# Attention in two groups per unit ahead of two feed-forward layers: rounds, corner masks, GpSimd low parts and early products

## The chip, the cores and the metric

The kernel runs on one core of a Trainium2 chip. The metric is the device time of one execution in microseconds. Before the change the median of three runs was 858.65 us (858.62 to 858.83).

## The reference

Three stages follow each other; everything is float32.

```python
# attention: 4 batches, 8 heads, 576 positions, 64 dimensions; stride 32
scores = q @ k.transpose(0, 1, 3, 2) / np.sqrt(64)
rel = pos[:, None] - pos[None, :]
mask_local = (rel >= 0) & (rel < 32)                                  # heads 0 to 3
mask_strided = (rel >= 0) & (pos[None, :] % 32 == pos[:, None] % 32)  # heads 4 to 7
attn = softmax(where(mask, scores, -1e9)) @ v
x = attn as 2304 tokens x 512
h = x @ w_in                       # 512 x 2048
y = (h * np.cos(h)) @ w_out        # 2048 x 512
g = y @ w_gate; val = y @ w_val    # 512 x 1536 each
out = (g / (1 + np.exp(-g)) * val) @ w_out2   # 1536 x 512
```

## The kernel before

**Engines.** TensorE multiplies; VectorE, ScalarE and GpSimd do what lies between; SP issues all loads, in the order in which the program writes them. Each engine works through its own instructions in the written order. The order is made by hand, in Python, by the loops below.

**Attention.** A unit is a batch with a pair of heads, either local or strided; 16 units, taken in pairs of one strided and one local unit. A local unit has nine blocks of 64 queries against 96 keys, a strided one eleven of 54 against 54. A unit is cut into three groups (`groups`, L78): three blocks each if local, four, four and three if strided. The loop at L813 runs in rounds. A round starts one group, strided and local in turn, so that a pair of units takes six rounds, and it takes the groups that were started earlier one step on: the sums, transpositions, values and puts of groups that are 2, 5, 6 and 7 rounds old (`LAGS`). The steps of a group: `scores` (TensorE; each float32 multiplication is two instructions in the trace, and the two heads lie in two 64x64 corners of the array; then a filler multiplication `hot` into unused columns, and one with an identity that adds the mask), `top` (VectorE's maximum, which GpSimd scales), `exps` (ScalarE), `sums` (VectorE), `norm` (VectorE's reciprocal, GpSimd's product), `transposes` (TensorE), `evac` (ScalarE), `values` (TensorE), `put` (ScalarE). Behind the last group, rounds go on for the older steps; these are the attention's tail. There TensorE gets a filler (`keep_warm`) or half of the first product of `x @ w_in`.

**Filler work.** `later` queues steps with a cost in units of about 1 us of VectorE, and `pump(share)` emits as many as a round's or slot's share allows; `need(key)` emits all that stands ahead of a key. In the attention the queue holds, for each of the 16 chunks of w_in, a conversion to float32 with a maximum (`conv_steps`: ScalarE, then VectorE); then the common scale; then the split of each chunk into a 16-bit high part (`hi`, ScalarE) and low part (`lo`, VectorE), with a scan of a chunk of w_out beside each. Chunk j+2's tile holds chunk j in float32 until j is split. Chunks (512 KB) arrive in six `raw` buffers; a step that frees one issues the next load. Loads of w_out wait for `RELEASE`.

**First layer.** `up1` multiplies block 0 to 4 of the tokens (512 or 384) with chunk m of w_in: 4 x 3 multiplications, high and low parts. A slot is one such product. On its result work `up1_a` (ScalarE, into one of four `tb` buffers), `up1_b` (VectorE), `up1_c` (ScalarE, the sine), `up1_d` (VectorE; frees the PSUM bank) and `up1_e` (ScalarE rounds, GpSimd subtracts for the low part; frees `tb`). The second multiplication, `down1` with w_out, starts at slot `HEAD`, and from there catches up at `RATE`. `direct_later` splits w_out beside it and scans w_gate and w_val. In slots ahead of `HEAD`, PSUM's four `acc` banks serve as further homes of products.

**Second layer.** It follows with the same weights' splits and isn't touched.

## Time and profile before

| | before |
|---|---|
| median of three runs | 858.65 us |
| the profiled execution's own time | 859.65 us |
| its span, first to last instruction | 858.0 us |
| TensorE busy | 844.9 us, 98% |
| VectorE, ScalarE, GpSimd busy | 653.6, 520.4, 200.0 us |
| TensorE's granted clock, mean | 1.000 |
| read from memory, written | 177.05, 23.99 MB |

A busy TensorE is not a TensorE at its peak: its instructions overlap, and the time between the starts of two is what one costs. So in the timeline below the difference of two rows' first column is read, not the second. The attention takes the first 100 us of the span; slot 16, where the second block begins, starts at 141 us.

### The profile page before, as it was taken

Reading aid. Unit: us, or ns where it says so; the run is one execution under the profiler, and the core shown is the slowest. Engines: PE = TensorE matmul, PEld = TensorE weight load, DVE = VectorE, ACT = ScalarE, POOL = GpSimd, SP = SyncE. Lnnn points to the kernel's source line nnn. Section 1 sums busy time; section 2 is a strip of 40 time slices with the busy share of each in tenths; the row PEclk is TensorE's granted clock in tenths of the full one; section 3 lists DMA queues with packets and bytes.
Section 4 is the critical chain, followed back from the end, with each engine's and each line's share of the span. In section 5 each row is a group of like instructions: output and inputs, shape, how many; then the busy total and the mean of one; then the engine's idle time right before and its main releaser. Section 6 shows DMA issues by size and latency. Waiting matters only on the chain.

```text
span 858.0 us, 18338 instructions
## 1 busy us (share of the span) xinstructions
PE 844.9 (98%) x7223; PEld 601.9 (70%) x7223; DVE 653.6 (76%) x1256; ACT 520.4 (61%) x1047; POOL 200.0 (23%) x281
## 2 busy tenths in 40 slices
PE   9999999999999999999999999999999999999998
PEld 5777544444444444555666788888888899999998
DVE  6999989997888978789996378567756765765562
ACT  6899889554657766768885466545344444444440
POOL 3454234211445546423223100000000000000000
PEclk9999999999999999999999999999999999999999
DMA  9998822897567566514356257667777688789894
GB/s 364 408 381 274 280 90 78 282 337 260 167 198 240 198 214 205 178 34 177 131 193 249 75 194 282 230 218 263 235 262 239 238 273 289 280 306 319 323 321 145
DMA packets 53605, 202.21 MB, mean 236 GB/s; under 512 B 5264, under 2 KB 15888, under 8 KB 49680
## 3 DMA queue, kind: packets, MB, share of 16 engines
q1 hardware_dynamic: 53520, 201.06, 67.3%
q8 instruction: 56, 0.92, 0.4%
q14 instruction: 29, 0.24, 0.1%
HBM read 177.05 MB, written 23.99 MB: 234 GB/s over the span
## 4 chain that ended last, share of the span: by engine, by line
PE 83%; DVE 11%; DMA 2%; ACT 2%; issue 1%; POOL 0%; SPq 0%; ACTq 0%; POOLq 0%
PE acc L734 14%; PE bank L581 13%; PE bank L582 12%; PE bank L583 12%; PE acc L583 7%; PE acc L581 7%; PE acc L582 7%; PE bank L466 3%; PE po L523 2%; DMA raw<-w_val 2%; DVE tb L624 1%; DVE tb L617 1%; PE tp L501 1%; DVE cv L265 1%; PE bank L468 1%
## 5 line engine op out<-in xcount | busy, mean ns | idle before, releaser
L581 PE MATMUL bank<-xs,wi 128*128 128x256 f16 (+3 forms) x776 | 231.1, 298 | 4.4 <-DVE q L145 1.7
L583 PE MATMUL bank<-xs,wi 128*128 128x256 f16 (+3 forms) x776 | 231.1, 298 | 0.0
L582 PE MATMUL bank<-xs,wi 128*128 128x256 f16 (+3 forms) x776 | 231.1, 298 | 0.0
L629 POOL TENSOR_TENSOR arena<-tb,arena 128x512 f16<-128x512 f32 (+1 forms) x80 | 91.5, 1144 | 239.6 <-ACT arena L628 212.9
L582 PEld LDWEIGHTS <-wi 128*128 128x128 f16 x880 | 86.1, 98 | 41.5 <-issue 7.2
L583 PE MATMUL acc<-arena 128*128 128x512 f16 (+1 forms) x320 | 114.5, 358 | 0.5 <-DVE arena L278 0.5
L581 PE MATMUL acc<-arena 128*128 128x512 f16 (+1 forms) x320 | 114.5, 358 | 0.0
L582 PE MATMUL acc<-arena 128*128 128x512 f16 (+1 forms) x320 | 114.5, 358 | 0.0
L581 PEld LDWEIGHTS <-wi 128*128 128x128 f16 x880 | 86.1, 98 | 36.0 <-issue 1.1
L583 PEld LDWEIGHTS <-wi 128*128 128x128 f16 x880 | 86.1, 98 | 34.7
L734 PEld LDWEIGHTS <-arena 128*128 128x128 f16 x1080 | 100.7, 98 | 8.1
L719 POOL TENSOR_TENSOR wi<-tb 128x256 f32<-128x256 f32 (+1 forms) x30 | 20.2, 675 | 338.5 <-DVE tb L701 338.5
L704 ACT ACTIVATE arena<-tb 128x256 f16<-128x256 f32 (+3 forms) x59 | 28.6, 485 | 99.0 <-DVE tb L701 90.6
L1228 DVE TENSOR_TENSOR arena<-bank,cv 128x512 f32<-128x512 f32 (+1 forms) x60 | 37.9, 636 | 66.0 <-PE bank L583 66.0
L583 PEld LDWEIGHTS <-arena 128*128 128x128 f16 x600 | 58.7, 98 | 33.7 <-DVE arena L278 1.0
L734 PE MATMUL acc<-arena 128*128 128x256 f16 (+1 forms) x702 | 82.0, 265 | 0.0
L582 PEld LDWEIGHTS <-arena 128*128 128x128 f16 x600 | 58.7, 98 | 32.6
L581 PEld LDWEIGHTS <-arena 128*128 128x128 f16 x600 | 58.7, 98 | 32.4
L628 ACT ACTIVATE arena<-tb 128x512 f16<-128x512 f32 (+1 forms) x80 | 46.6, 583 | 53.5 <-PE acc L583 51.9
L614 ACT ACTIVATE tb<-bank,quarter,c 128x512 int32<-128x512 f32 (+1 forms) x74 | 53.7, 725 | 33.7 <-PE bank L583 25.5
L701 DVE SCALAR_TENSOR_TENSOR tb<-tb,c,arena 128x512 f32<-128x512 f32 (+1 forms) x60 | 41.7, 695 | 35.8 <-ACT tb L696 35.8
L1224 ACT ACTIVATE cv<-bank 128x512 f32<-128x512 f32 (+1 forms) x90 | 49.3, 548 | 30.1 <-PE bank L583 29.1
(143 smaller groups left out, 1722.3 us busy)
## 6 DMA issues: line engine op xcount, KB each, us to landing
wi<-w SPq DMA_DIRECT2D x20, 1792.0 KB, 7.7
arena<-w SPq DMA_DIRECT2D x60, 576.0 KB, 4.9
raw<-w_out SPq DMA_DIRECT2D x56, 512.0 KB, 4.7
arena<-w SPq DMA_DIRECT2D x10, 1792.0 KB, 8.9
raw<-w_gate SPq DMA_DIRECT2D x24, 512.0 KB, 4.2
raw<-w_val SPq DMA_DIRECT2D x24, 512.0 KB, 5.6
w<-arena SPq DMA_DIRECT2D x42, 256.0 KB, 3.0
raw<-w_in SPq DMA_DIRECT2D x16, 512.0 KB, 9.1
```

The lines of the kernel that those rows point to most:

```text
L466: nc.tensor.matmul(out=self.sc[r, i, :], lhsT=qk_t[self.i][r, q0:q0 + 64], rhs=qk_t[self.i][r, k0:k0 + w], start=i == 0, stop=False)
L581: nc.tensor.matmul(out=o, lhsT=w[:, 0, c], rhs=x[0], start=first, stop=False, **kw)
L582: nc.tensor.matmul(out=o, lhsT=w[:, 0, c], rhs=x[1], start=False, stop=False, **kw)
L583: nc.tensor.matmul(out=o, lhsT=w[:, 1, c], rhs=x[0], start=False, stop=last, **kw)
L614: nc.scalar.activation(out=c["w"].bitcast(I32), in_=c["ph"], func=AF.Identity, scale=turn[c["blk"]], bias=quarter)
L628: nc.scalar.activation(out=g[:, 0, 0:n], in_=w, func=AF.Copy)
L629: nc.gpsimd.tensor_tensor(out=g[:, 1, 0:n], in0=w, in1=g[:, 0, 0:n], op=ALU.subtract)
L701: nc.vector.scalar_tensor_tensor(out=t, in0=t, scalar=s_g[c["blk"]], in1=c["C"][m][:, 1, 0:c["n"]], op0=ALU.mult, op1=ALU.mult)
L704: nc.scalar.activation(out=to, in_=src, func=AF.Copy, scale=2.0 ** -11)
L734: nc.tensor.matmul(out=o[:, c], lhsT=w[:, 256 * i + 128 * c:256 * i + 128 * c + 128], rhs=unit(u)[:, x:x + h], start=j == c == i == 0, sto ...
L1224: nc.scalar.activation(out=t, in_=src, func=AF.Copy)
L1228: nc.vector.tensor_tensor(out=c["C"][m][:, :, h * right:h * right + h], in0=p, in1=t, op=ALU.add)
```

## The change

Units are cut into two groups (five and four blocks if local, six and five if strided), so a pair of units takes four rounds instead of six. The lags are 2, 4, 5 and 6. In `scores` the filler comes first and has the columns that the group leaves free; the mask is added by two multiplications, each in the corner of its head. In a round, scores come ahead of transpositions, exponentials ahead of evictions, and VectorE's maximum stands between two halves of the filler work. A strided and a local group share one tile of sums and one reciprocal. There are three tiles of exponentials of each kind instead of four. The values of a pair of units are loaded in its first round, before they were in the round ahead of it. The low parts of w_in's odd chunks are made on GpSimd in two instructions. In the tail four whole first products are multiplied instead of one in halves. Shares and limits of the filler work have other numbers. `AHEAD` is 0 and adds only three empty steps.

```diff
-LAGS = (2, 5, 6, 7)
+LAGS = (2, 4, 5, 6)
+ROUND = 4
-PUMP, KP = 1.05, 8
+PUMP, PUMP_END, KP = 1.25, 2.2, 5
-EARLY, K0 = 1, 1
-HEAD, HSHARE = 16, 0.8
-RATE, MINLAG = 0.7, 2
+EARLY, K0 = 4, 2
+HEAD, HSHARE = 17, 0.8
+RATE, MINLAG = 0.75, 2
-RELEASE = 30
+RELEASE = 18
...
-    return [(0, 3), (3, 3), (6, 3)] if is_local(p) else [(0, 4), (4, 4), (8, 3)]
+    return [(0, 5), (5, 4)] if is_local(p) else [(0, 6), (6, 5)]
...
+            def lo_pool(mat, j, tiles):
+                c = as_f32(tiles[j + 2])
+                nc.gpsimd.tensor_scalar(out=c, in0=c, scalar1=scale_w[mat][0], scalar2=1.0, op0=ALU.mult, op1=ALU.mult)
+                nc.gpsimd.tensor_tensor(out=tiles[j][:, 1], in0=c, in1=tiles[j][:, 0], op=ALU.subtract)
+
             def lo(mat, j, tiles):
-                later(0.7, lambda: lo_part(tiles[j][:, 1], as_f32(tiles[j + 2]), scale_w[mat][0], tiles[j][:, 0]), (mat, j))
+                if j % 2:
+                    later(0, lambda: lo_pool(mat, j, tiles), (mat, j))
+                else:
+                    later(0.7, lambda: lo_part(tiles[j][:, 1], as_f32(tiles[j + 2]), scale_w[mat][0], tiles[j][:, 0]), (mat, j))
...
+                nc.tensor.matmul(out=b[:, n * w:512], lhsT=ones16, rhs=hot[:, 0:512 - n * w], start=True, stop=False)
...
-                nc.tensor.matmul(out=b[:, 288:512], lhsT=ones16, rhs=hot[:, 0:224], start=False, stop=False)
-                nc.tensor.matmul(out=self.sc, lhsT=id16, rhs=mask, start=False, stop=True)
+                for h in range(2):
+                    r = slice(64 * h, 64 * h + 64)
+                    nc.tensor.matmul(out=self.sc[r], lhsT=id16[r, r], rhs=mask[r], start=False, stop=True)
...
             if group(LAGS[0]):
-                group(LAGS[0]).sums()
+                mate = group(LAGS[0] + 1)
+                group(LAGS[0]).sums(mate)
+                if group(LAGS[0]).loc:
+                    group(LAGS[0]).invert()
+                    mate.norm()
+                    group(LAGS[0]).norm()
+            if group(0):
+                group(0).scores()
+            begun = k - len(gs) - K0
+            if 0 <= begun < EARLY:
+                need(("in", begun))
+                early = up1(0, begun)
...
+            share = 0 if k < KP else PUMP if group(0) else PUMP_END
+            pump(share * 0.5)
+            if group(0):
+                group(0).top()
+                if g == 0 and i >= 4:
+                    load_v(i)
+                    load_v(i + 1)
...
+            pump(share * 0.5)
```

TensorE, two rounds in the middle of the attention, as the program orders them: first a local round of before, from its transpositions on (`tp`; `bank` holds scores, `po` values, `fix` the masks). A float32 multiplication is one row here and two instructions in the trace.

```order
L505 MATMUL tp<-fix,e_s_100 128x128 x2
L466 MATMUL bank<-qkl 64x96 x6
L468 LDWEIGHTS ones_77
L468 MATMUL bank<-hot,ones_77 128x224
L469 LDWEIGHTS id_76
L469 MATMUL bank<-fix,id_76 128x288
L523 MATMUL po<-pt,vl 64x64 x6
```

And a local round of the change:

```order
L472 MATMUL bank<-hot,ones_77 128x32
L478 MATMUL bank<-qkl 64x96 x10
L482 LDWEIGHTS id_76
L482 MATMUL bank<-fix,id_76 64x480
L482 LDWEIGHTS id_76
L482 MATMUL bank<-fix,id_76 64x480
L521 MATMUL tp<-fix,e_l_103 96x128 x5
L541 MATMUL po<-pts,v_pair_107 64x54 x12
```

Of what was three rounds' work of a unit two rounds are left; the filler stands first and is short, and the mask is in two halves of 64 partitions.

ScalarE in the attention's tail, from the first high parts of w_in on (`wi<-wi`; `xy<-po` are puts, `pt` and `pts` evictions, `tb` the first steps of products). Before:

```order
L275 ACTIVATE wi<-wi,s_1681 128x512 x2
L545 ACTIVATE xy_68<-po 128x8x12
L545 ACTIVATE xy_69<-po 128x8x6
L512 ACTIVATE pts<-tp 128x256
L481 ACTIVATE e_s_98<-bank,mx 128x54 x3
L275 ACTIVATE wi<-wi,s_1681 128x512
L536 ACTIVATE xy_69<-po 128x192
L512 ACTIVATE pt<-tp 96x384
L481 ACTIVATE e_l_102<-bank,mx 128x96 x3
L545 ACTIVATE xy_69<-po 128x12x6
```

With the change:

```order
L278 ACTIVATE wi<-wi,s_1688 128x512 x4
L554 ACTIVATE xy_70<-po 128x256
L530 ACTIVATE pt<-tp 96x384
L530 ACTIVATE pt<-tp 96x256
L278 ACTIVATE wi<-wi,s_1688 128x512 x2
L563 ACTIVATE xy_69<-po 128x18x6
L563 ACTIVATE xy_70<-po 128x18x12
L530 ACTIVATE pts<-tp 128x384
L632 ACTIVATE tb<-bank,quarter,c_1770 128x512
L278 ACTIVATE wi<-wi,s_1688 128x512 x2
L554 ACTIVATE xy_69<-po 128x192
L554 ACTIVATE xy_70<-po 128x128
```

The first high parts stood ahead of groups that still had their exponentials to come; now they stand behind all exponentials, more of them per round, and among the first products' steps.

SP's loads ahead of the third pair of units' values (`v_pair`, `vl`), from the fourth pair's queries and keys on (`qks`, `qkl`). Before:

```order
L432 DMA qks<-qk_s 128x1188
L432 DMA qkl<-qk_l 128x1184
L195 DMA raw<-w_in 128x1024 x2
L443 DMA v_pair_108<-v_s 64x768 x2
L439 DMA vl<-v_l 128x1152
```

With the change:

```order
L443 DMA qks<-qk_s 128x1188
L443 DMA qkl<-qk_l 128x1184
L198 DMA raw<-w_in 128x1024 x2
L443 DMA qks<-qk_s 128x1188
L443 DMA qkl<-qk_l 128x1184
L198 DMA raw<-w_in 128x1024
L454 DMA v_pair_106<-v_s 64x768 x2
L450 DMA vl<-v_l 128x1152
```

The fifth pair's queries and keys and one more chunk of w_in have moved ahead of the values.

## Rows read from the trace of the kernel before

**Rows 1.** Windows: stretch, its length, busy us (instructions) per engine, clock, DMA share, GB/s

```profile
20.00:90.00 70.00, 69.93 (x1177) 50.40 (x1173) 66.67 (x192) 65.03 (x245) 34.99 (x75) 1.00 0.94 351
141.00:208.00 67.00, 65.51 (x303) 29.51 (x303) 63.36 (x110) 37.97 (x60) 13.76 (x13) 1.00 0.84 294
```

**Rows 2.** Chain of waits: start us, us, engine, tile, line

```profile
71.80 0.52 PE po L523 x12
...
111.71 0.78 ACT tb L614
...
113.08 1.16 POOL arena L629
114.30 0.78 ACT tb L614
```

**Rows 3.** TensorE's timeline: two rounds from 42.99 us; start, us, instructions

```profile
42.99 0.56 PE L466 MATMUL bank<-qks 64*64 64x54 f32 x12
43.48 0.27 PE L468 MATMUL bank<-hot,ones 128*128 128x224 bf16 x1
43.59 0.23 PE L469 MATMUL bank<-fix,id 128*128 128x162 bf16 x1
43.75 0.56 PE L523 MATMUL po<-pts,v_pair 108*64 108x54 f32 x12
44.24 0.44 PE L505 MATMUL tp<-fix,e_s 128*128 128x128 f32 x2
44.61 0.71 PE L466 MATMUL bank<-qkl 64*64 64x96 f32 x12
...
46.54 0.67 PE L466 MATMUL bank<-qks 64*64 64x54 f32 x16
47.14 0.27 PE L468 MATMUL bank<-hot,ones 128*128 128x224 bf16 x1
```

**Rows 4.** Last two score multiplications of 43 us; line L466's durations (min/median/max ns)

```profile
43.32 0.23 PE L466 MATMUL bank<-qks 64*64 64x54 f32 x2
...
L466 PE MATMUL bank<-qks x12: 218/218/258, 43.0 to 43.3; 64*64 64x54 f32 x12
```

**Rows 5.** TensorE's timeline: the first scores, and the first instruction behind the last round

```profile
6.43 1.10 PE L466 MATMUL bank<-qks 64*64 64x54 f32 x16
...
91.26 0.33 PE L811 MATMUL bank<-fix,id 128*128 128x384 bf16 x1
```

**Rows 6.** DMA, 0 to 100 us: GB/s in 40 slices of 2.5 us; loads, KB each

```profile
GB/s 57 385 380 405 412 420 420 400 415 406 406 408 404 407 410 409 405 412 404 416 401 410 314 264 411 416 372 197 288 243 164 228 321 331 308 246 231 228 257 297
...
raw<-w_in SPq DMA_DIRECT2D x16, 512.0 KB, 9.1
qks<-qk_s SPq DMA_DIRECT2D x8, 594.0 KB, 8.6
...
vl<-v_l SPq DMA_DIRECT2D x8, 576.0 KB, 7.4
v_pair<-v_s SPq DMA_DIRECT2D x16, 192.0 KB, 6.6
```

**Rows 7.** ScalarE's timeline from 104.73 us

```profile
104.73 1.28 ACT L621 ACT_TABLE_LOAD   x1
...
106.65 0.76 ACT L614 ACTIVATE tb<-bank,quarter,c 128x512 int32<-128x512 f32 x1
107.32 0.71 ACT L275 ACTIVATE wi<-wi,s 128x512 f16<-128x512 f32 x1
107.93 0.71 ACT L621 ACTIVATE tb<-tb,right 128x512 f32<-128x512 f32 x1
```

**Rows 8.** VectorE's timeline: two low parts of w_in, the second beside GpSimd

```profile
91.35 0.74 DVE L278 SCALAR_TENSOR_TENSOR wi<-wi,s 128x512 f16<-128x512 f32 x1
92.01 0.68 DVE L204 TENSOR_REDUCE pw_out<-raw 128x1 f32<-128x512 f32 x1
...
92.95 1.18 DVE L278 SCALAR_TENSOR_TENSOR wi<-wi,s 128x512 f16<-128x512 f32 x1
```

More of the change, by code (lines that the diff above doesn't have):

```diff
@@ L164, in build @@
         beside = {j: [] for j in range(M1)}
+        ahead = [("gate", j) for j in range(AHEAD)]
         for i, key in enumerate((mat, j) for mat in ("gate", "val") for j in range(M2)):
-            beside[ALONE + i * (M1 - ALONE) // (2 * M2)].append(key)
-        order = deque([("in", j) for j in range(M1)] + [("out", j) for j in range(M1)]
+            if key not in ahead:
+                beside[ALONE + i * (M1 - ALONE) // (2 * M2)].append(key)
+        order = deque([("in", j) for j in range(M1)] + [("out", j) for j in range(M1)] + ahead
                       + [key for j in range(M1) for key in [("out", j)] + beside[j]]
@@ L774, in quarter_out @@
                 store("12", 0, h)
-        gs = [Group(i + d, g) for i in range(0, len(units), 2) for g in range(3) for d in range(2)]
+        gs = [Group(i + d, g) for i in range(0, len(units), 2) for g in range(2) for d in range(2)]
         load_qk(0)
@@ L804, in build @@
         scale_later(TW_IN, "in")
[L805 removed]
+        split_chain([("in", j, wi) for j in range(M1)], 2, lambda j: scan_later("out", j - M1 + 16) if j > M1 - 16 else None)
+        for j in range(16, M1):
+            scan_later("out", j)
+        top_later("out")
         steps = deque()
         def keep_warm():
[L810 removed]
+            t = bank()[:, 0:5 * LW].rearrange("p (n w) -> p n w", w=LW)
             nc.tensor.matmul(out=t, lhsT=id16, rhs=ml, start=True, stop=True)
@@ L815, in group @@
                 return gs[k - lag] if 0 <= k - lag < len(gs) else None
-            i, g = 2 * (k // 6), k % 6
+            i, g = 2 * (k // ROUND), k % ROUND
             if group(LAGS[0]):
-                group(LAGS[0]).sums()
+                mate = group(LAGS[0] + 1)
[10 more added lines that the diff above has]
+                early = up1(0, begun)
+            elif not group(0) and begun < 0:
+                keep_warm()
             if group(LAGS[1]):
                 group(LAGS[1]).transposes()
-            if group(0):
-                group(0).scores()
-                group(0).top()
-            begun = k - len(gs) - K0
-            if 0 <= begun < 2 * EARLY:
-                m = begun // 2
-                if begun % 2 == 0:
-                    need(("in", m))
-                    early = up1(0, m, range(KC // 2))
-                else:
-                    up1(0, m, range(KC // 2, KC), early)
-                    up1_a(early)
-                    steps.append((0, m, early))
-            elif not group(0):
-                keep_warm()
             if group(LAGS[3]):
                 group(LAGS[3]).put()
+            if group(1):
+                group(1).exps()
             if group(LAGS[1]):
@@ L841, in build @@
                 group(LAGS[2]).values()
-            if group(0) and g == 5:
-                for j in (i + 2, i + 3):
-                    if i and j < len(units):
-                        load_v(j)
-                for j in (i + 6, i + 7):
-                    if j < len(units):
-                        load_qk(j)
-            if group(1):
-                group(1).exps()
-            pump(PUMP if k >= KP else 0)
-            if group(LAGS[0]):
-                group(LAGS[0]).norm()
+            if 0 <= begun < EARLY:
+                up1_a(early)
+                if steps:
+                    up1_b(steps[-1][2])
+                    up1_c(steps[-1][2])
+                if len(steps) > 1:
+                    up1_d(steps[-2][2])
+                steps.append((0, begun, early))
+            share = 0 if k < KP else PUMP if group(0) else PUMP_END
[5 more added lines that the diff above has]
+                    load_v(i + 1)
+                if g == ROUND - 1:
+                    for j in (i + 6, i + 7):
+                        if j < len(units):
+                            load_qk(j)
+            pump(share * 0.5)
             if k >= RELEASE:
@@ L994, in build @@
         opened, most = [], [HOMES]
+        for mat, j in ahead:
+            scan_later(mat, j, 0.75)
+        for _ in range(3):
+            later(1.0, lambda: None)
         for j in range(M1):
@@ L1065, in build @@
                     urge(scale_pieces([1, 2, 3], sy, 2))
-                c = up1(blk, m, spare=slot // 2 % KC if slot % 2 and slot < HEAD - 4 else None)
+                c = up1(blk, m, spare=slot // 2 % KC if slot % 2 and EARLY < slot < HEAD - 4 else None)
                 if blk == NBLK - 1 and m in (7, 14):
```

62 lines of the change are left out of this document (33 added, 29 removed).

## The prediction

> **What bounds the kernel now.** I read the windows first. While the attention runs, TensorE is busy without a gap at the full clock (granted 1.00, the level of 2.4 GHz), and VectorE, ScalarE and the DMA queues stand at 95%, 93% and 0.94 beside it [rows 1]: four resources with almost the same limit. The chain of waits of the same stretch names TensorE up to 71.8 us. Behind the attention it leaves TensorE, although that engine shows no gap there either. From 111.7 us it goes round a loop [rows 2]: ScalarE's first step on a product (`up1_a`, L614), the rounding of an older one (L628), GpSimd's low part (L629), and ScalarE again. The reason is in the code: `up1_a` of product s writes a `tb` buffer, there are four, and GpSimd's low part of product s-4 is what frees it. One turn takes 2.59 us (111.71 to 114.30), of which 1.16 are GpSimd's. A product's twelve multiplications of 512 columns need as long on TensorE (2.56 us at 2.4 GHz), so nobody can catch up: when `up1_a` of product 4 begins (111.71) decides when block 1 begins. This is the step that I follow.
>
> **TensorE's part of the change.** The timeline gives the price of a round [rows 3]. Sixteen score multiplications take 0.60 us from start to start, twelve take 0.49: 0.0275 each and 0.16 for the segment itself. In the same way the mask is its columns at 2.4 GHz plus 0.09 (162 columns, 0.16), the filler of 224 columns 0.11 (0.02 of its own), the values 0.16, the transpositions 0.18 plus some 0.1 each (two, 0.37). A round thus costs 0.61 us whatever is in it. A pair of units is 1.62 + 2 x 1.86 + 3 x 1.93 = 11.1 us now (a strided round of three blocks, two of four, three local ones). Scores, values and transpositions stay as they are; two rounds of six go (-1.22), and the filler shrinks from 1344 to 590 columns (-0.31). The masks keep 1458 columns. Whether two corners run side by side decides if they cost the same or 0.61 more: two score multiplications of 54 columns together span 0.23 us where one has 218 ns [rows 4], so the second begins within 0.012 us, less than the 0.0225 that 54 columns need. They overlap, and I take no difference. A pair becomes 9.6 us; eight pairs save 12.2.
>
> The last round of scores ended at 91.26 before, begun at 6.43 [rows 5]. The same sum (eight pairs without the transpositions and values that the first rounds lack, 5.3 us) gives 83.7 where 84.8 were measured, 1.3% more. For the change: 76.8 - 5.7 = 71.1, with that share 72.0, so 78.4.
>
> **DMA.** The queues ran full until 55 us [rows 6]. The values of the third pair of units are now loaded at the start of their pair, and in SP's queue one more of the 512 KB w_in loads and a pair's queries stand ahead of them: five pairs of 2 x 594 KB, two of 384 + 576 KB, nine loads of w_in, the first 384 KB and the constants are 13.3 MB, which the row has moved by 35 us. The multiplication that needs them comes in round 13, about 6.4 + 4.5 (four rounds of scores alone) + 1.6 + 8 x 2.4 + 2 = 33.7. A wait of 1.3 us, and everything else on TensorE is queued behind it. Bounds: none (if ScalarE was late anyway) to 4 (if SP is held by a buffer). So the scores end at 79.7; call this E.
>
> **ScalarE's tail.** Before, the split of w_in stood beside the last seven rounds of scores and the eight behind them. Now it starts only at E, since 27 rounds at PUMP 1.25 are 34 units of filler work where 40 at 1.05 were 42, and all sixteen chunks are split ahead of `up1_a` of product 4. ScalarE's work between: sixteen high parts of 0.61 us, 9.8; four `up1_a` of 0.67, 2.7; three sines as long as a high part, 1.9; the table load, 1.3; one rounding, 0.5 of the 0.7 us until GpSimd starts on it [rows 2, 7]; puts, evictions and the last exponentials, 17 instructions at the attention's mean of 0.27 [rows 1], 4.5. Together 20.7. Queued among them are waits that the change adds: the high part of chunk j+2 overwrites the memory that holds chunk j, so it waits for the low part of j, and for odd j that is GpSimd's now, in two instructions. The second is like L629, 1.16. The first has no row: no more than the two-input one (1.16), no less than nothing; one input instead of two, so I take 0.8. With the semaphores 2.05 us, for each odd chunk. Followed by hand, ScalarE waits 1.3 us ahead of chunk 3, 1.3 ahead of 5 (two normalisations stand in front) and 1.5 ahead of 15, since the `up1` steps in between give GpSimd time. Behind these waits stand the evictions that TensorE's next transpositions need; it has 2.6 us of `up1` to cover them in each of four rounds. Last, chunk 15's low part (2.05) and the first rounding's (1.16) stand in GpSimd's queue ahead of product 4, 3.3 us with a semaphore. Sum: 20.7 + 4.1 + 3.3 = 28.1 behind E, 107.8.
>
> VectorE and GpSimd also meet. A low part on VectorE takes 0.74 us, but 1.18 where GpSimd multiplies beside it [rows 8]. The eight even ones now run beside a GpSimd that is hardly ever idle. Bounds: nothing (they fall into its waits) to 8 x 0.44 = 3.5; only the ones before chunk 7 lie on the loop, so I take 0.8. The trace so agrees with the Trainium skill, SBUF — State Buffer, section "Who interferes with whom", by which a VectorE instruction with two SBUF inputs and a GpSimd one that reads SBUF exclude each other for a whole instruction.
>
> Product 4 then begins at 108.6 instead of 111.71: -3.1.
>
> **What costs nothing, and under which cover.** VectorE gives 6 us of odd low parts to GpSimd (8 x 0.74) and loses 32 of 48 reciprocals and 32 of 96 reductions: it is not the last in the new tail, where GpSimd and ScalarE cover what it has left. The four early products take 8 us of TensorE out of the head, but the head goes by the loop, so they fill time. HEAD 17 starts the second projection one slot later, with 2.4 units more of VectorE's work left at slot 16. VectorE has 3.6 us idle from 141 to 208 [rows 1], which hides it; without that cover it costs up to 2.4. From there to the end nothing changes.
>
> **The sum** against the profiled span of 858.0 us (that execution's own time was 859.65, 1.0 above the median of 858.65): -3.1, so 855.5 for the median. No change is within 0.2% (856.9 to 860.4), about what a measurement of this kernel can tell.
>
> **The rivals.** (A) The loop doesn't hold, since ScalarE and GpSimd run further ahead than I think: the 12.2 us of rounds arrive whole but for the 1.3 of DMA, and the waits of the tail shrink by half. -8 to -11, 849. For it: TensorE is all of the chain to 71.8. Against it: the loop's 2.59 us.
> (B) No gain: the head's gain is given back between 141 and 208, where VectorE is busy 63.4 of 67 us and the forced steps (`need`) now come with four units of debt instead of three. 2.4 of the 3.1 go, 858.
> (C) Slower: GpSimd's low parts are the bound of the tail. The place is ScalarE's wait ahead of each odd high part. If the pair of instructions takes 3.0 instead of 2.05 us (1.16 for the first, and each blocked by a VectorE low part of 0.66), the eight odd chunks follow each other at 3.7 us, 2.9 + 8 x 3.7 + 3.3 = 35.8 behind E, 7.7 more: 862. It decides from 2.45 us on, where the gain is gone.
> (D) The corners don't run together. Then 0.61 x 8 = 4.9 us of the 12.2 are lost, and the gain with them: 860. The row of two starts within 0.012 us speaks against it. By the Trainium skill, TensorEngine Tiling (Array Packing), "Gotcha 1: PSUM Pressure", different row tiles can't access one PSUM bank at the same time, and these two do write one bank; so do the score multiplications that the trace shows together.
>
> **Numbers.** The small gain (853 to 857) gets 0.47, A 0.14, B 0.18, C 0.16, D 0.05. Predicted is the first, 855.5. For eight in ten the range goes from half of A to a third of C: 848.5 to 861. Faster: 0.42 of the first and A, 0.56. Same: 0.05 of the first, 0.14 of B, 0.04 of C, 0.03 of D, 0.26. Slower 0.18.
>
> **What would show it.** The step between local scores and the next hot filler: 9.6 us per pair of units, and the two mask corners starting together. The last scores' round ends near 80 us. TensorE waits for v_pair's load about 34 us. In the tail ScalarE waits for GpSimd's low part of w_in ahead of an odd high part, and `up1_a` of product 4 starts at 108 to 109, ahead of GpSimd's L629 loop. TensorE then idles some 5 us in the last slots of block 0, because it ran ahead and the banks are not read. From slot 17 on everything is as before, 3 us earlier. The prediction is wrong if product 4 starts before 105 or after 112, if the first GpSimd instruction takes more than 1.2 us, or if TensorE waits for low parts of w_out by more than 2 us in all.

## The result and the profile after

The changed kernel takes 869.29 us (median of 4 runs, 868.82 to 872.07) where the one before, on the same chip, takes 858.74. The ratio is 1.0124, with an interval of 1.0112 to 1.0136: slower by 10.6 us. The profiled execution took 868.82 us with a span of 867.0, so 9.0 of span are to be found (858.0 before; that execution lay 0.9 above its median, and this one 0.5 below).

TensorE's timeline of the changed kernel: the start of two successive pairs of units (57.02 and 66.83), and some of its waits (the last bracket is the idle time ahead of the row and what ended it).

```profile
57.02 0.28 PE L472 MATMUL bank<-hot,ones 128*128 128x242 bf16 x1
57.23 0.79 PE L478 MATMUL bank<-qks 64*64 64x54 f32 x20
57.85 0.28 PE L482 MATMUL bank<-fix,id 64*64 64x270 bf16 x2
...
66.83 0.28 PE L472 MATMUL bank<-hot,ones 128*128 128x242 bf16 x1
...
74.07 0.55 PE L521 MATMUL tp<-fix,e_s 128*128 128x128 f32 x3 [0.99 <-POOL e_s L513]
...
82.53 0.79 PE L541 MATMUL po<-pts,v_pair 108*64 108x54 f32 x20
84.73 0.22 PE L145 MATMUL bank<-tops,ones 128*128 128x128 bf16 x1 [1.41 <-DVE tops L139]
...
130.06 0.27 PE L145 MATMUL bank<-tops,ones 128*128 128x128 bf16 x1 [4.31 <-DVE tops L139]
...
147.22 0.38 PE L599 MATMUL bank<-xs,wi 128*128 128x512 f16 x1 [1.57 <-DVE tb L642]
...
228.69 0.27 PE L145 MATMUL bank<-tops,ones 128*128 128x256 bf16 x1 [2.11 <-DVE tops L139]
```

Two corners of a mask span 0.28 us (57.85), and one of 270 columns alone lasts 275 ns by the durations of its line: they run side by side. A pair of units takes 9.81 us (57.02 to 66.83). The last round of scores ends at 83.3 (82.53 + 0.79), 8 us ahead of the kernel before [rows 5]. Slot 16 begins at 147.22, 5.9 behind the 141.31 of before; the other 3.1 are lost behind it. From 149 to 232 TensorE waits 5.0 us in all, the 2.11 at 228.69 being the longest; in the kernel before it waits 2.0 from 143 to 225.

ScalarE from the last exponentials (L494) to the head's loop:

```profile
86.05 1.04 ACT L494 ACTIVATE e_l<-bank,mx 128x96 f32<-128x96 f32 x4 [1.55 <-POOL mx L488]
...
87.33 1.35 ACT L278 ACTIVATE wi<-wi,s 128x512 f16<-128x512 f32 x2
...
90.76 0.72 ACT L278 ACTIVATE wi<-wi,s 128x512 f16<-128x512 f32 x1 [1.14 <-POOL wi L304]
...
96.04 0.72 ACT L278 ACTIVATE wi<-wi,s 128x512 f16<-128x512 f32 x1 [3.04 <-POOL wi L304]
...
113.26 0.72 ACT L278 ACTIVATE wi<-wi,s 128x512 f16<-128x512 f32 x1 [1.14 <-POOL wi L304]
113.89 0.61 ACT L646 ACTIVATE arena<-tb 128x512 f16<-128x512 f32 x1
117.16 0.78 ACT L632 ACTIVATE tb<-bank,quarter,c 128x512 int32<-128x512 f32 x1 [2.66 <-POOL arena L647]
...
122.30 0.78 ACT L632 ACTIVATE tb<-bank,quarter,c 128x512 int32<-128x512 f32 x1 [0.67 <-POOL arena L647]
...
124.87 0.78 ACT L632 ACTIVATE tb<-acc,quarter,c 128x512 int32<-128x512 f32 x1 [0.66 <-POOL arena L647]
```

The first high part comes 4.0 us behind the scores' end. The scale that it needs is ready 3.0 us behind it, by VectorE's timeline:

```profile
86.16 0.15 DVE L121 TENSOR_SCALAR s<-s 128x1 f32<-128x1 f32 x1
```

The last microsecond goes to the last exponentials and an eviction, which stand ahead of the high part on ScalarE. The waits for GpSimd's low parts (L304) ahead of odd high parts are there, and so is the one ahead of `up1_a` of product 4, which begins at 117.16 where 111.71 was before [rows 2]. Then the loop goes on at 2.57 us a turn.

The windows of the tail, and of the clock behind TensorE's wait of 4.31 us:

```profile
83.30:87.33 4.03, 2.02 (x27) 1.44 (x25) 3.35 (x9) 2.48 (x10) 1.52 (x3) 1.00 0.60 225
87.33:117.16 29.83, 25.69 (x185) 12.76 (x186) 22.62 (x37) 20.45 (x38) 17.89 (x19) 1.00 0.69 233
...
126.00:128.00 2.00, 0.00 (x0) 0.00 (x0) 1.62 (x3) 1.34 (x3) 1.16 (x1) 1.00 0.00 0
128.00:130.00 2.00, 0.00 (x0) 0.00 (x0) 1.69 (x5) 1.34 (x4) 1.16 (x1) 0.51 0.00 0
130.00:132.00 2.00, 1.94 (x6) 0.82 (x6) 1.76 (x7) 1.91 (x3) 0.63 (x1) 0.50 0.00 0
132.00:134.00 2.00, 2.00 (x7) 0.64 (x5) 1.36 (x4) 1.44 (x3) 0.59 (x2) 0.50 0.00 0
134.00:136.00 2.00, 2.00 (x10) 0.86 (x9) 0.12 (x1) 1.14 (x2) 1.09 (x1) 0.78 0.00 0
```

ScalarE (the fourth busy number) works 20.45 of the 29.83 us; no engine is full there (TensorE, the first, has 25.69). While TensorE waited, its granted clock fell from 1.00 to 0.50, the level of 1.2 GHz, and the next product took 5.1 us instead of 2.59.

### The profile page after: what moved, and what is told of

Same layout as the page of the kernel before. It is cut to its first block, busy times and chain, and to the rows that moved or that the text cites. A ratio compares the mean times of both kernels' runs of the same rounds, so it can differ in the third digit from the quotient of the medians.

```text
span 867.0 us, 18118 instructions
## 1 busy us (share of the span) xinstructions
PE 836.8 (97%) x7219; PEld 598.7 (69%) x7219; DVE 644.8 (74%) x1184; ACT 517.7 (60%) x1019; POOL 211.5 (24%) x262
## 4 chain that ended last, share of the span: by engine, by line
PE 76%; DVE 10%; DMA 7%; ACT 4%; issue 2%; POOL 1%; SPq 0%; POOLq 0%; ACTq 0%
PE acc L752 14%; PE bank L599 12%; PE bank L600 12%; PE bank L601 12%; PE acc L601 7%; PE acc L599 7%; PE acc L600 7%; DMA qks<-qk_s 3%; DMA raw<-w_val 2%; DVE xs L281 1%; DMA v_pair<-v_s 1%; PE bank L478 1%; PE po L541 1%; DVE tb L635 1%; DVE cv L268 1%
## 5 line engine op out<-in xcount | busy, mean ns | idle before, releaser
L599 PE MATMUL bank<-xs,wi 128*128 128x256 f16 (+3 forms) x784 | 234.1, 299 | 7.0 <-DVE tb L642 4.3
L600 PE MATMUL bank<-xs,wi 128*128 128x256 f16 (+3 forms) x784 | 234.1, 299 | 0.5 <-DVE xs L281 0.5
L601 PE MATMUL bank<-xs,wi 128*128 128x256 f16 (+3 forms) x784 | 234.1, 299 | 0.0
L647 POOL TENSOR_TENSOR arena<-tb,arena 128x512 f16<-128x512 f32 (+1 forms) x80 | 93.7, 1172 | 219.6 <-ACT arena L646 210.2
L1259 ACT ACTIVATE cv<-bank 128x512 f32<-128x512 f32 (+1 forms) x90 | 49.3, 548 | 30.1 <-PE bank L601 29.1
```

The lines of the kernel that those rows point to most:

```text
L599: nc.tensor.matmul(out=o, lhsT=w[:, 0, c], rhs=x[0], start=first, stop=False, **kw)
L600: nc.tensor.matmul(out=o, lhsT=w[:, 0, c], rhs=x[1], start=False, stop=False, **kw)
L601: nc.tensor.matmul(out=o, lhsT=w[:, 1, c], rhs=x[0], start=False, stop=last, **kw)
L647: nc.gpsimd.tensor_tensor(out=g[:, 1, 0:n], in0=w, in1=g[:, 0, 0:n], op=ALU.subtract)
L1259: nc.scalar.activation(out=t, in_=src, func=AF.Copy)
```

## The experiments

All times are medians against the kernel before in the same comparison (858.7 to 859.2 each time). "Product 4" is the start of `up1_a` of product 4 (117.2 in the changed kernel, 111.7 before), "slot 16" the start of that product on TensorE (147.2 and 141.3). In the expectations the fifth product is product 4. Each filler step has a cost in the queue (`later`), and an edit that changes a cost also changes how many steps a round emits; where that bears on a reading, it is said.

**Theories.** 1: the split of w_in, from its scale to the last high part, is one serial chain; it used to start 12 us ahead of the scores' end, starts 4 us behind it now, and the head's loop carries the lateness to slot 16. 2: GpSimd's low parts are what makes it long. 3: the pace of the second projection (HEAD, RATE) loses the time. 4: VectorE or the clock, not the loop, set slot 16.

### GpSimd's low parts

In the changed kernel, taken back:

```diff
-                if j % 2:
+                if False:
```

> The changed kernel with all low parts of w_in on VectorE again. Theory 1 (the split of w_in is one serial chain that now starts behind the last scores instead of 12 us ahead of them; whatever lies in it delays the head one to one): ScalarE's 5.3 us of waits for GpSimd ahead of high parts and the 2.7 ahead of the fifth product go, VectorE's 6 us more fall mostly into the 8 us that it waits there; the fifth product's first step comes at 112 to 114 instead of 117.2, time 864 to 867. Rival 2 (GpSimd's low parts are the loss, as in case C): the fifth product comes before 109 and the time is 862 or less. Rival 3 (the loss is the pace of the second projection): 869, no change.

865.52, ratio 1.0076 (1.0059 to 1.0093). ScalarE and TensorE:

```profile
112.08 0.78 ACT L632 ACTIVATE tb<-bank,quarter,c 128x512 int32<-128x512 f32 x1 [1.27 <-POOL arena L647]
...
126.71 0.71 ACT L278 ACTIVATE wi<-wi,s 128x512 f16<-128x512 f32 x1
...
150.56 0.39 PE L599 MATMUL acc<-arena 128*128 128x512 f16 x1 [2.61 <-ACT arena L278]
```

Product 4 at 112.1, slot 16 at 139.7: as theory 1 said. Not all of the 5.1 us is GpSimd's speed: an odd low part costs 0.7 in the queue now and cost nothing on GpSimd, so the split is spread out, and three of its sixteen high parts come behind product 4, the last at 126.71. But slot 16 is now ahead of the kernel before by 1.6 us and the time is 6.7 behind: TensorE waits 2.61 us at 150.56 for the first chunk of w_out (`ACT arena L278`), and its clock is 0.57 from 152 to 156. Of 7.5 us at slot 16 only 3.8 reach the end.

The reverse, in the kernel before: `lo_pool` for odd chunks and nothing else.

> The kernel before with w_in's odd low parts on GpSimd in two instructions and nothing else. Theory 1: the split stands beside the last scores here, ScalarE has evictions and exponentials to do while GpSimd works, and VectorE (19.5 of 20 us busy from 80 to 100) gets 6 us free; the fifth product between 110 and 113, time 857 to 860. Rival 2 (GpSimd's pair behind its normalisations is too slow anywhere): the fifth product 3 to 5 us later than 111.7, TensorE waits for normalisations from 80 us on, time 861 to 864.

872.47, 1.0157 (1.0140 to 1.0174): 13 us lost by this edit alone, where theory 1 expected next to nothing. Rival 2 was right in direction and too small. GpSimd's timeline shows it:

```profile
87.44 1.11 POOL L503 TENSOR_TENSOR e_l<-e_l,ls 128x288 f32<-128x288 f32 x1
88.53 0.19 POOL L483 TENSOR_SCALAR mx<-mx 128x4 f32<-128x4 f32 x1
88.68 0.54 POOL L503 TENSOR_TENSOR e_s<-e_s,ls 128x216 f32<-128x216 f32 x1
89.20 0.19 POOL L483 TENSOR_SCALAR mx<-mx 128x3 f32<-128x3 f32 x1
89.38 0.69 POOL L300 TENSOR_SCALAR wi<-wi,s 128x512 f32<-128x512 f32 x1
90.15 1.15 POOL L301 TENSOR_TENSOR wi<-wi 128x512 f16<-128x512 f32 x1
91.26 1.11 POOL L503 TENSOR_TENSOR e_l<-e_l,ls 128x288 f32<-128x288 f32 x1
```

No row has a wait: from 81.5 to 92.3 GpSimd goes without a pause, a chunk and two normalisations in 3.8 us, and the normalisation of a local group takes 1.11 us here where 0.67 is its median. Product 1 waits for the attention's end until 106.21 (101.09 before) and then runs at a clock of 0.50 to 0.55 until 110. Slot 16 is 7.2 us late (148.51). The rest is lost at the scale of w_gate and w_val, and the clock behind it is 0.50 from 216 to 222:

```profile
217.71 0.37 PE L144 MATMUL bank<-tops,ones 128*128 128x256 bf16 x1 [4.12 <-DVE tops L138]
```

Here too the queue's pace changed with the engine: the odd low parts cost it nothing, and the last high part begins at 105.22 instead of 110.25. How much of the 13 us this denser filler made, and how much GpSimd's order, is not separated.

### When the split starts

PUMP 1.6 instead of 1.25 in the changed kernel:

> The changed kernel with PUMP 1.6 instead of 1.25, so that the 34 units of filler ahead of the split are out after 21 rounds instead of 27. Theory 1: the first high part of w_in comes 6 to 8 us earlier (79 to 81 instead of 87.3); VectorE was full from 20 to 60 us, so the rounds get longer and the last scores end 2 to 3 us later, and the fifth product comes 3 to 5 us earlier; time 864 to 866. Rival 2 (GpSimd's low parts): the eight pairs follow each other as slowly as now, time 868 to 870. Rival 3: 869.

874.68, 1.0183 (1.0163 to 1.0203): worse, outside of every expectation. The first high part came at 80.1, as expected, but the last scores began at 94.8 instead of 81.6. The windows show the first of three places where it is lost:

```profile
58.00:62.00 4.00, 4.00 (x85) 3.14 (x79) 3.27 (x7) 3.65 (x12) 0.52 (x2) 1.00 1.02 407
62.00:64.00 2.00, 0.34 (x5) 0.22 (x2) 1.68 (x4) 2.00 (x9) 1.29 (x2) 0.93 1.04 409
64.00:74.00 10.00, 10.00 (x112) 7.64 (x111) 9.35 (x18) 7.51 (x25) 3.78 (x7) 0.50 0.47 171
74.00:78.00 4.00, 4.00 (x80) 3.17 (x77) 3.80 (x9) 3.40 (x15) 1.71 (x3) 1.00 0.93 304
```

TensorE waits 1.66 us for a normalisation, to 63.8, and then runs 10 us at 0.50. Two more waits for normalisations, 2.51 us at 85.34 and 2.00 at 100.50, are followed by 0.50 as well. Denser rounds cost more than the earlier start gains: in the changed kernel VectorE was busy for 39.5 of the 40 us from 20 to 60 already.

A shorter way to an earlier start: each w_in chunk's maximum over half of its columns.

```diff
-                nc.vector.tensor_reduce(out=part, in_=box["h"].bitcast(F32), op=ALU.max, axis=AX.X, apply_absolute_value=True)
+                nc.vector.tensor_reduce(out=part, in_=box["h"].bitcast(F32)[:, 0:256], op=ALU.max, axis=AX.X, apply_absolute_value=True)
...
-            return box, [(0, g0)] + [(0.63, g1)] * scan + ([(0.55, g2), (0.85, g3)] if mat in ('gate', 'val') else [(0.36, g2), (0.63, g3)])
+            return box, [(0, g0)] + [(0.36, g1)] * scan + ([(0.55, g2), (0.85, g3)] if mat in ('gate', 'val') else [(0.36, g2), (0.63, g3)])
```

> The changed kernel with the maximum of a w_in chunk taken over half of its columns (left out of the computation: the other half of the scan), at 0.36 instead of 0.63 units. The filler ahead of the split is 4.3 units shorter, 3.5 rounds. Theory 1 (the split starts too late): first high part at 79 to 81 instead of 87.3, the last scores within 2 us of now (81.6 begin of the last multiplication), the fifth product at 110 to 113, time 863 to 866. Rival (the tail is as long wherever it begins, since high parts among the scores delay the exponentials): the scores end 4 us later or more and the fifth product stays at 116 to 118, 867 to 870.

867.59, 1.0094 (1.0078 to 1.0110). The first high part comes at 81.8, 5.5 us earlier, and product 4 at 117.0, where it was. The earlier start is not passed on, as the rival said. Its mechanism is not shown: the last scores begin 2.6 us later and not 4, and that delay is older than the first high part. The rounds are 2.0 us behind at 64 us, and TensorE waits 1.76 us for a normalisation at 66.78. ScalarE's longest waits ahead of odd high parts are 1.83 and 3.44 us (1.14 and 3.04 in the changed kernel), and TensorE's clock is 0.50 from 90 to 98, with a wait of 2.70 us in between.

The same half scan with low parts on VectorE:

> The changed kernel with low parts on VectorE and the maximum of a w_in chunk over half its columns (the other half of the scan is left out of the computation). The run with half maxima alone started the split 5.5 us earlier and gained nothing at the fifth product (117.0), because GpSimd's queue set the pace. If it is GpSimd that made the tail long wherever it began, then without it an earlier start comes through: fifth product at 106 to 109 (112.1 with the low parts moved alone), slot 16 at 134 to 137, and the time, by VectorE's 5 us less work, 859 to 863. If the tail is one chain of ScalarE and VectorE whatever its start, the fifth product stays at 111 to 113 and the time at 864 to 866.

865.83, 1.0083 (1.0069 to 1.0097). TensorE and ScalarE:

```profile
66.04 0.65 PE L521 MATMUL tp<-fix,e_s 128*128 128x128 f32 x3 [1.77 <-POOL e_s L513]
...
81.01 1.35 ACT L278 ACTIVATE wi<-wi,s 128x512 f16<-128x512 f32 x2
...
115.04 0.78 ACT L632 ACTIVATE tb<-bank,quarter,c 128x512 int32<-128x512 f32 x1 [1.27 <-POOL arena L647]
```

Product 4 at 115.04, later than the 112.1 of the low parts alone, although the split started 7 us earlier, at 81.01. So theory 1's first half is not borne out: an earlier start alone does not bring product 4 earlier, with the low parts on either engine. The reason is not isolated. The last scores begin at 84.3 instead of 82.4, but that delay was there before any high part: TensorE waits 1.77 us at 66.04 and its clock is 0.57 from 66 to 70. It then loses 2.1 us at the lower clock from 92.6 on, and 2.6 from 146.5. The profiled execution took 868.17 us, 2.3 above the median, so its product 4 may be later than usual.

### The head's loop

The rounding and the low part (`finish`) ahead of `up1_a`, in the changed kernel and in the one before:

```diff
+                if len(steps) > 2:
+                    finish(steps.popleft())
                 up1_a(c)
                 up1_b(steps[-1][2])
-                if len(steps) > 2:
-                    finish(steps.popleft())
```

> The changed kernel with the rounding and the low part of the third product back written ahead of up1_a in each slot, so that GpSimd works while ScalarE makes its first step; no other change. Theory 1 with the loop of the prediction (up1_a, rounding, GpSimd, up1_a, 2.57 us a turn for products of 2.59): the fifth product still comes at 117, but a turn then takes what ScalarE has to do, about 2.0 to 2.2 us, slot 16 starts at 141 to 143 instead of 147.2, TensorE's wait of 4.3 us at 130 shrinks and with it the stretch at the lower clock; time 863 to 866. If the loop isn't what carries the lateness to slot 16 (rival 4: VectorE or the clock do), slot 16 stays within 1 us of 147 and the time at 868 to 870.

864.80, 1.0069 (1.0054 to 1.0084): 4.5 us back. ScalarE's timeline:

```profile
118.05 0.78 ACT L632 ACTIVATE tb<-bank,quarter,c 128x512 int32<-128x512 f32 x1 [2.14 <-POOL arena L647]
...
119.86 0.77 ACT L632 ACTIVATE tb<-acc,quarter,c 128x512 int32<-128x512 f32 x1
...
121.65 0.77 ACT L632 ACTIVATE tb<-bank,quarter,c 128x512 int32<-128x512 f32 x1
```

Product 4 is no earlier (118.05), but a turn takes 1.8 us instead of 2.57, without a wait for GpSimd, and slot 16 comes at 142.8. The wait of 4.31 us shrinks to 1.84, and the product behind it runs at the full clock. Rival 4 is out: the loop carried the lateness to slot 16.

> The kernel before with the rounding and low part of the third product back ahead of up1_a. By the prediction the loop set the head of this kernel too, 2.57 us a turn; but TensorE's products need 2.59 and it never waits there, so by theory 1 nothing can come sooner than the products: 858 to 859, no change. If the loop did hold the head of the kernel before, slot 16 comes 2 to 5 us earlier than 141.3 and the time is 854 to 857.

858.25, 0.9991 (0.9981 to 1.0000), slot 16 at 140.5. In the kernel before, TensorE's own products came at the loop's pace, so there is little to gain; about a microsecond may be real, which the interval doesn't settle. With HSHARE 0.9 on top:

> The kernel before with the rounding and low part ahead of up1_a (858.25 alone, 0.9991) and HSHARE 0.9 instead of 0.8, so that the slots of the head emit 12% more filler. VectorE is idle for 2.9 us from 100 to 141 there; if its balance up to the scale of w_gate and w_val sets the time, 1 to 2 us of that come back, 856 to 858. If more filler delays the products' own steps, TensorE waits in the head and the time is 859 to 862.

860.98, 1.0024 (1.0014 to 1.0034): slower, although the scale of w_gate and w_val came 1.5 us earlier yet (213.7). More filler in the head has its price elsewhere.

### The pace, the early products, and all together

```diff
-HEAD, HSHARE = 17, 0.8
-RATE, MINLAG = 0.75, 2
+HEAD, HSHARE = 16, 0.8
+RATE, MINLAG = 0.7, 2
```

> The changed kernel with HEAD 16 and RATE 0.7 as before the change. Theory 1: slot 16 starts at 147 as it does now, and of the 3 us that are lost between 150 and 230 none to 2 come back, since they go with VectorE's and the loads' lateness: 867 to 869. Rival 3 (the pace of the second projection): the 3 us behind slot 16 and some of the idle time ahead of it come back, 865 or less. Rival 2: 869.

866.98, 1.0096 (1.0081 to 1.0111): 2.3 us back, with slot 16 where it was (146.9). TensorE's waits between 149 and 232 fall from 5.0 to 2.7 us, and the 2.11 ahead of the scale's multiplication at 228.69 are among those that go. HEAD and RATE went back together; which of them did it is not shown.

> The changed kernel with the three edits that each gained: low parts on VectorE, HEAD 16 and RATE 0.7, and the rounding and low part ahead of up1_a. If the three losses are apart from each other (tail, loop, pace; -3.8, -4.5, -2.3 us measured one by one) the sum is 858.7, the time of the kernel before; then TensorE's 8.7 us of earlier scores would still be unpaid. If they share one limit (VectorE from 141 to 230), 861 to 864. Fifth product's first step at 112, slot 16 at 136 to 138.

863.90, 1.0057 (1.0035 to 1.0079). Product 4 at 111.6 and slot 16 at 136.5, as expected, and still 4.7 us slower than before: the three gains (3.8, 4.5 and 2.3 one by one) do not add up. In the profiled execution (865.55 us) TensorE waits 2.22 us for the first chunk of w_out at 144.95 and 1.96 at 186.83, each followed by 1.6 us of loss at the lower clock. Two other executions had a mean clock of 1.000 and took 861.87 and 862.44 us, still some 3 us behind the kernel before, so the clock is not all of it.

> As the run with three edits undone or moved (863.9), but with HEAD 17, so that the second projection begins one product later, with RATE 0.7. If TensorE's wait of 2.2 us for the first chunk of w_out at 145 and the 1.5 us at the lower clock behind it are what eats that version's earlier head, both go and the time is 859 to 861. If VectorE's balance sets it (195 us of work up to the scale of w_gate and w_val, wherever TensorE waits), the wait comes back later and the time is 863 to 865.

864.73, 1.0062 (1.0046 to 1.0077), no better. Where its waits lie is not shown.

The low parts on VectorE with one early product (EARLY 1 instead of 4):

> The changed kernel with low parts on VectorE and one first product in the tail instead of four. If the early products' steps (three up1_a, three up1_b, three sines among the high parts) are what is left of the longer tail, the high parts end 3 to 5 us earlier than with four; but the products start later, product 1 at 100 to 104 and slot 16 at 140 to 143 (139.7 with four), time 864 to 868. If VectorE's work is the bound (below), nothing changes by more than 1 us: 865 to 866.5.

863.41, 1.0055 (1.0040 to 1.0070), 2.1 better than with four. ScalarE:

```profile
110.45 0.78 ACT L632 ACTIVATE tb<-bank,quarter,c 128x512 int32<-128x512 f32 x1
```

The last high part comes at 109.7 instead of 126.7, product 4 at 110.5 and slot 16 at 137.8, earlier than expected: the early products' steps on ScalarE and VectorE did stand ahead of the split.

> The changed kernel with low parts on VectorE, one early product, HEAD 16 and RATE 0.7, and the rounding and low part ahead of up1_a: of the change there remain the two groups, the corner masks, the shared reciprocal and the filler's shares. Fifth product at 108 to 110.5, slot 16 at 134.5 to 136.5, 5 us ahead of the kernel before. If VectorE's balance up to the scale of w_gate and w_val sets the time (195 us of work as before, 10 us more of waits), TensorE waits 4 to 6 us behind slot 16 and the time is 860 to 863. If the remaining loss of 863.4 was only the pace and the loop, it is 855 to 858.

859.01, ratio 0.9998 (0.9988 to 1.0008): all four edits taken back or moved (the fourth is the order of `finish`, which the change had left alone) give the time of the kernel before. What remains of the change, mainly two groups, corner masks, the shared reciprocal and the shares, gains nothing, although slot 16 begins at 135.6, 5.7 us ahead. Its fair partner is the kernel before with the same order of `finish` (0.9991); their intervals overlap, so no gain is shown against that either.

### What eats the 5.7 us behind slot 16

The scans of w_out, w_gate, w_val and w_out2 over half of the columns, in that kernel and in the one before:

```diff
-            nc.vector.tensor_reduce(out=parts_w[mat][:, i:i + 1], in_=src, op=ALU.max, axis=AX.X, apply_absolute_value=True)
+            nc.vector.tensor_reduce(out=parts_w[mat][:, i:i + 1], in_=src[:, 0:256], op=ALU.max, axis=AX.X, apply_absolute_value=True)
...
-        def scan_later(mat, j, cost=0.63):
+        def scan_later(mat, j, cost=0.36):
...
-                scan_later(mat, i, 0.75)
+                scan_later(mat, i, 0.45)
```

> The same with the maxima of w_out, w_gate, w_val and w_out2 taken over half of each chunk's columns (the other half of these scans is left out of the computation): some 12 us less VectorE work up to the scale of w_gate and w_val. If VectorE is what eats the rounds' gain, TensorE's waits behind slot 16 go, the scale comes 8 to 12 us earlier and the time falls to 850 to 855, below the kernel before. If the waits are latencies of a chain that VectorE's work doesn't lengthen, it stays within 2 us of the run beside it.

863.46, 1.0048 (1.0032 to 1.0063).

> The kernel before with the same half scans left out. TensorE is its bound (9 us idle in all), so no more than the 2 to 3 us that it waits between 140 and 220 can come back: 855.5 to 858.5, although the scale of w_gate and w_val may come 4 to 8 us earlier. If VectorE bounds this kernel as well, 852 to 855.

862.86, 1.0043 (1.0027 to 1.0059). Both are 4 us slower, although the 40 scans ahead of the scale of w_gate and w_val take 16.3 us of VectorE instead of 27. So less work on VectorE does not help by itself; the steps' costs fell with it, so their order on the engines changed too, and the two were not separated. The scale comes earlier, at 207.05 instead of 220.4 and at 208.5 instead of 216.5, but TensorE pays for it, as its waits in the first of the two show, and the window behind them:

```profile
207.05 0.37 PE L145 MATMUL bank<-tops,ones 128*128 128x256 bf16 x1 [3.56 <-DVE tops L139]
207.94 0.58 PE L599 MATMUL bank<-xs,wi 128*128 128x512 f16 x1 [0.51 <-DVE q L146]
```

```profile
208.00:213.00 5.00, 5.00 (x12) 1.66 (x12) 2.93 (x8) 0.00 (x0) 0.00 (x0) 0.50 0.37 115
```

The scale's multiplication stands in TensorE's order where the filler's credit put it, and there TensorE waits for it and is slow behind it. In the kernel before with half scans the same wait is 1.63 us (0.81 without the edit), and the clock is 0.50 from 210 to 212.

Four and two chunks of w_gate loaded ahead of w_out's second load (AHEAD 4 and 2), which fills the pause of the queues from 118 to 139 us:

> The changed kernel with the four edits taken back (859.0, slot 16 at 135.6) and AHEAD 4: four chunks of w_gate are loaded and scanned ahead of the second load of w_out. Theory: what TensorE is ahead at slot 16 (5.7 us) is given back since everything from there waits on one stream of loads, 24 MB from 141 to 208 us at 350 GB/s, that doesn't start sooner because all six raw buffers are held until slot 16 (no load from 118 to 139). With four loads moved into that pause 6 us of the stream are gone: TensorE's waits at 182 and 188 (2.5 us in sum) go, the scale of w_gate and w_val comes 4 to 8 us earlier than 220.4, time 855 to 857.5. If it is VectorE's order of instructions and not the loads, the four scans (2.6 us) delay the products' own steps and the split of w_out, and the time is 859 to 861.

858.97, 0.9995 (0.9986 to 1.0004).

> The same with two chunks: half of each, 856.5 to 858.5 by the theory of the loads, 859 to 860 by the other.

860.10, 1.0016 (1.0007 to 1.0025). The waits at 182 and 188 us shrink or go, as the theory of the loads said, and nothing is won: in both, TensorE now waits 2.0 us for w_out's first chunk (at 143 us), and with four chunks it is slow behind it, which costs 1.6 us more. TensorE's waits of the two kernels, grouped by what ended them, from 134 us with AHEAD 0 and from 136 with AHEAD 4 (sum, times, longest):

```profile
PE acc L601 <- DVE arena L281: 2.9, 4, 1.9
PE bank L599 <- DVE tb L642: 1.9, 1, 1.9
PE bank L599 <- DVE q L146: 0.6, 1, 0.6
```

```profile
PE acc L599 <- ACT arena L278: 2.0, 1, 2.0
PE acc L601 <- DVE arena L281: 1.6, 3, 1.0
PE bank L599 <- DVE q L146: 0.6, 1, 0.6
```

A wait that is taken away in one place is found in another: at the split of w_out (`arena`), at a product's step that frees a PSUM bank (`tb`, L642), or at a scale (`q`).

## Why the prediction was wrong

Predicted was 855.5, between 848.5 and 861; it became 869.3. The step that failed is the start of product 4: it was to come at 108.6 and came at 117.16, past the 112 that the prediction named as its own refutation, since the split's start at E, ScalarE's tail with GpSimd's low parts and the four early products were priced too low. Moving the low parts back brought product 4 to 112.1, and one early product instead of four, on top of that, to 110.5. A second step failed behind it: "from there to the end nothing changes", where 3.1 us more were lost. Step by step:

- **A round's price: right.** A pair of units takes 9.8 instead of 9.6 us where no wait disturbs it, and the corners run together, so rival D is out. The rule cited with it (the Trainium skill, TensorEngine Tiling (Array Packing), "Gotcha 1: PSUM Pressure") does not hold for these two tiles in one bank: 0.28 us for two where one has 275 ns.
- **The end of the scores: 83.3 instead of 79.7.** The DMA term was too large (the wait for v_pair showed as 0.5 us on the weight loads at 36 us, not 1.3). Missing were waits for normalisations, 1.75 us at 68 to 80 and 0.92 at 13.5, and two more in the first 20 us (0.77 for the masks' identity, 0.35 for an eviction). I took the full TensorE of [rows 1] as a bound that would stay one when its work shrank; VectorE and ScalarE, at 95 and 93% beside it, had no room to follow.
- **"Now it starts only at E": the first failure of size.** The split began 4.0 us behind E. The scale of w_in is a chain of its own (maximum, TensorE, maximum, reciprocal) that ended 3.0 us behind E, the last exponentials and an eviction took the rest, and I gave both no time. (The half maxima show that an earlier start alone is not passed on.)
- **ScalarE's tail: right in its work, near in its waits.** Work was 20.45 us against 20.7, waits 9.4 (29.83 - 20.45) against 4.1 + 3.3 + 0.8. The two misses and these add up: 3.6 + 4.0 + 1.2 - 0.3 = 8.5 of the 8.6 us by which product 4 was late. That says where the time lies, not what would give it back; by the runs, the low parts' move returned 5.1 of the 8.6 and the early products 1.6 more.
- **The loop: right, and confirmed by taking it away.** From product 4 to slot 16 it took 30.1 us, 29.6 before. A prediction that sees such a loop must fear a late start more than it hopes for an early one. That the loop alone held the kernel before is not borne out: without it slot 16 moved by 0.8 us.
- **HEAD 17 "hides": wrong cover, right size.** I gave 2.4 as its cost without cover; taking HEAD and RATE back gave 2.3. The 2.3 are for two edits, so the agreement is in part luck. VectorE's 3.6 idle us from 141 to 208 were no cover as far as they are waits: 1.9 for the multiplication of a scale on TensorE and 1.2 for loads of w_val.
- **Rival C: right in its sign, wrong in its condition.** The pair of instructions took 1.95 us when undisturbed (0.70 and 1.16) and 2.37 at most, so the point of 2.45 was never passed. What cost time was the queue: normalisations and low parts in one order on GpSimd. In the longest wait, 3.04 us, the low part stood behind two normalisations, which had themselves waited 1.41 us for VectorE's reciprocal. Some of these instructions were lengthened where VectorE and GpSimd met: one of eight first instructions (1.13), and three of VectorE's eight low parts (1.62, 1.16 and 1.30 from 0.75, together 1.8 us). It agrees with the Trainium skill, SBUF — State Buffer, "Who interferes with whom"; I had priced the lock on VectorE alone, at 0.8 us, and GpSimd, "hardly ever idle" in the prediction, worked 17.89 of the tail's 29.83 us.
- **Four early products "fill time": wrong.** Their steps stand ahead of high parts on ScalarE and VectorE. One instead of four gained 2.1 us.
- **Rival B was right in its kind.** The lead over the kernel before at slot 16 (5.7 us with all four edits) was given back behind it; of what an edit won there against the changed kernel, a part arrived (3.8 of 7.5 us for the low parts).
- **The clock had no term.** The prediction expected TensorE to idle some 5 us in the last slots of block 0, and it waited 4.31 at 130.06, but the 2.3 us that the product behind it lost at the lower clock were not in the sum. With the loop turned round, the wait was 1.84, and the clock stayed at 1.00.

Of the 10.6 us, the runs give 3.8 to the low parts, 2.3 to the pace, 2.1 to the early products and 4.5 to the loop that carries lateness, each measured singly or on top of the first; they overlap, since together they return 10.3 and not 12.7. Shown is that these four edits together give back the loss. The turned loop is not a part of the change, and no run takes back the other three alone; by an estimate from the runs (863.4 with low parts and early products moved, 2.3 for the pace) they would leave some 861. Open is why two groups gain nothing in what remains: the waits behind slot 16 move from step to step, and neither less scanning nor earlier loads took them away. That a tighter order of these steps could win the 5.7 us was not tried. Nor was a run without the three empty steps, which the change puts ahead of w_out's split at a cost of 1.0 each and which stand in every run of the changed kernel.

## What to carry to other kernels

Here three engines stood at 93 to 100%, and work taken from one of them moved the wait and didn't shorten the run; ask first which chain the others have to finish, and by when. Before a step is given to an idle engine, look at what stands in that engine's queue at that moment and who waits for it: 0.75 us on VectorE became 1.95 on GpSimd, ahead of normalisations that TensorE needs, and the move, with the free place in the filler queue that came with it, cost 13 us in the kernel before. A buffer loop whose turn is as long as the bound's own can't recover a delay; changing the order of two steps so that the other engine works in between took 0.8 us off each turn, without a byte of memory.

## What the runs showed of the hardware

- TensorE's clock made small waits dear. In a wait of 4.31 us, to 130.06, the granted clock fell to 0.50, the level of 1.2 GHz, and stayed there past 134 us; after one of 1.66 us (PUMP 1.6) it was 0.50 for 10 us. Not every wait of that size did it: behind 1.84 us (`finish` first), 1.88 (all four edits) and 1.98 (AHEAD 2) it stayed at 1.00. In the kernel before, where no wait behind the first 2 us is longer than 1.1, it was 1.00 in every window up to 800 us.
- GpSimd's instructions are lengthened beside VectorE's two-input ones, and not only VectorE's beside GpSimd: a normalisation of 0.67 us took 1.11 (87.44, `lo_pool` in the kernel before), a one-input multiplication of 128 x 512 took 1.13 instead of 0.69 (93.64 in the changed kernel).
- Two 64x64 multiplications in opposite corners, which write the same PSUM bank, run side by side also in bf16: two of 270 columns span 0.28 us where one lasts 275 ns, and two of 480 span 0.37 where one lasts 363.
